# Decay on the attention output, a closer second layer, new planning figures, and load tiles kept at multiples of 256 bytes, in a fused attention and MLP kernel

## The chip, the cores and the metric

The kernel runs on one core of one Trainium2 chip. The metric is the device time of one execution in microseconds (us). An execution counts as slow when it took over 1.5% longer than the fastest of the same kernel. Ratios and profiles use runs in the fast state alone. Three executions were in the slow state (one of e2 at 218.12 us, one of e3 at 216.13, one of the kernel before at 751.23); they are in the medians and ranges that I quote, not in the ratios. The profile covers a slightly shorter stretch than the timed run (span 212.4 us against 214.5 us timed), so spans are compared with spans and times with times. In the profile's lines PE is TensorE (PEld its weight loads), DVE VectorE, ACT ScalarE, POOL GpSimd, and a q behind a name is that engine's sequencer. SBUF and PSUM are the memories that the kernel's tiles lie in; every matmul here writes its result to PSUM. An eviction is the copy of such a result from PSUM to SBUF.

## The reference, cut to what matters

```python
batch, n_heads, seq, head_dim = (4, 8, 768, 64); block = 64
rel = pos[:, None] - pos[None, :]
Dmask = np.where(rel >= 0, lam[:, None, None] ** rel[None, :, :], 0.0)
# for each block of the sequence:
intra = np.einsum('bhic,bhjc->bhij', qb, kb) * Dmask[None]
intra = np.einsum('bhij,bhjd->bhid', intra, vb)
inter = np.einsum('bhid,bhde->bhie', qb * lam_pow[None], kv_state)
out[:, :, sl] = intra + inter
kv_state = lam_block * kv_state + np.einsum('bhsd,bhse->bhde', kb * rev_pow[None], vb)
# then an MLP on x = attention output, 3072 x 512 -> 2048 -> 512
h = x @ w_in
g = np.where(h >= 1, h, np.where(h <= -1, 0.0, (h + 1) ** 2 / 4))
y = g @ w_out
```

The decay lam^(i-j) is a product of a factor of the query's position, lam^i, and one of the key's, lam^(-j). The kernel multiplies V (which carries the key's index) by the key's factor on GpSimd. The query's factor belongs to one row of the result, so it may be applied to the query or, just as well, to the finished output row. That freedom is what the change uses.

## The kernel before

There are 24 blocks of 128 tokens. The first six are transposed on TensorE, the 18 later ones by a DMA. Their outputs become xT, the input of layer 1: 96 groups of matmuls (16 of 128 columns each for the first three of six stages, then 8 of 256). Layer 2 has 96 groups of four matmuls of 512 columns (the last four groups in two pieces each). Between the layers ScalarE makes r = relu(h+1), and VectorE makes t = min(r/2, 1), w = r - t and gT = w*t, one set for every two layer-1 groups.

```python
def f_qn(c):        # query of a later block, scaled on VectorE: two SBUF inputs
    nc.vector.tensor_tensor(kq[c % NKQ][:, 2 * HP:, :]..., qkv_ld[c, 0],
                            _bc(tab_n[:, c % NCB, :], 2, D), op=AX.mult)
def f_qT(c):        # query of one of the first six blocks, scaled out of PSUM
    nc.vector.tensor_tensor(qT[c], ptt[c][1], tab_q[:, c % NCB], op=AX.mult)
def f_m(c, g):      # mask of the scores, PSUM times SBUF -> sc
    ...
def f_o(c):         # output matmuls, po <- sc,vi and the state's part
    ...
def f_x(c):         # eviction of the attention output, plain copy on ScalarE
    nc.scalar.copy(out=xT[sx][:, :, off:off + C], in_=pot[c])
```

No engine's program is written down in order. Every operation is added to a list with its planned duration, what it needs and when it is due; a list scheduler runs over these planned times and emits each engine's instructions in the order that comes out. A changed duration in the plan therefore moves real instructions.

```python
l_seq = [(1,) + x for x in l1_order[:FO]]        # FO = 16 layer-1 groups first
for i in range(len(l2_order)):                   # then one of each in turn
    l_seq.append((2,) + l2_order[i])
    if i + FO < len(l1_order):
        l_seq.append((1,) + l1_order[i + FO])
...
# in the scheduler: where TensorE is planned to wait, it gets matmuls on zeros
for _ in range(int((t - pe_end - 60) // (216 if t > 8000 else 430))):
    nc.tensor.matmul(spin, lhsT=idle[:, 0:128], rhs=idle, start=True, stop=True)
```

The last loop makes the "fillers": matmuls whose result nobody reads.

## Time and profile before

| | before |
|---|---|
| time, median of 3 runs | 213.78 us (213.44 to 214.03) |
| span of the profile | 212.4 us |
| busy: TensorE, VectorE, ScalarE, GpSimd | 205.3, 160.2, 150.4, 116.1 us |
| VectorE between 45 and 104 us | 55.92 of 59.00 us |
| gaps of TensorE after 18.3 us | 2.14 us |
| fillers after 18 us | 4 |

The page's summary of the chain that ended last is the first thing to read, as shares of the span by engine:

```profile
PE 66%; DVE 21%; DMA 6%; issue 3%; POOL 2%; ACT 1%; POOLq 0%; DVEq 0%
```

VectorE holds 21% of the chain. That says how long one could walk back through VectorE's instructions, not how much time is lost there: the chain may go along whichever of two full engines happens to end last. The lines that show how little TensorE really loses are in the prediction.

### The profile page before, as it was taken

The numbers are of one execution on the slowest core, as the hardware profiler recorded it, in microseconds if no ns is written. First come the engines' busy times: TensorE is split into PE (matmuls) and PEld (weight loads), VectorE is DVE, ScalarE is ACT, GpSimd is POOL, SyncE is SP. The second block draws the span as 40 slices with busy tenths as digits, with TensorE's granted clock in tenths as the row PEclk, the third lists the DMA queues.
The fourth block names the chain that finished last, engine by engine and source line by source line (L and its number), as shares of the span: only waits on it lengthen the run. The fifth ranks groups of instructions, "written<-read, shape, count | busy, mean of one in ns | idle before, by whom it ended". The sixth has DMA issues, their size and how long they took to land.

```text
span 212.4 us, 5710 instructions
## 1 busy us (share of the span) xinstructions
PE 205.3 (97%) x2324; PEld 146.7 (69%) x2324; DVE 160.2 (75%) x240; ACT 150.4 (71%) x306; POOL 116.1 (55%) x148
## 2 busy tenths in 40 slices
PE   7899999999999999999999999999999999999994
PEld 2476987676649788779677767667767776666442
DVE  6627887899997999999999999798769546364200
ACT  5899785498749898868789887795977664444120
POOL 8998636159998798687377586673835000000000
PEclk9999999999999999999999999999999999999999
DMA  5999999999999999894997969978861400110112
GB/s 143 258 224 244 213 262 265 220 219 189 269 274 261 253 216 155 205 257 104 204 229 172 205 142 235 221 167 198 205 154 43 124 25 27 49 49 34 68 49 99
DMA packets 95737, 36.80 MB, mean 173 GB/s; under 512 B 87392, under 2 KB 91744, under 8 KB 95712
## 3 DMA queue, kind: packets, MB, share of 16 engines
q1 hardware_dynamic: 90064, 28.06, 58.6%
q0 software_dynamic: 5504, 8.39, 18.3%
q8 instruction: 18, 0.29, 0.6%
q14 instruction: 7, 0.06, 0.1%
q10 hardware_dynamic: 144, 0.00, 0.0%
HBM read 27.27 MB, written 6.29 MB: 158 GB/s over the span
## 4 chain that ended last, share of the span: by engine, by line
PE 66%; DVE 21%; DMA 6%; issue 3%; POOL 2%; ACT 1%; POOLq 0%; DVEq 0%
PE ph L385 29%; PE py L430 29%; DVE w L403 5%; DVE gT L418 4%; DVE t L399 4%; DVE kq L276 4%; DMA w_in_sb<-in_moe_w_in_dram 4%; DVE kq L273 2%; DMA x1f<-in_k_dram 2%; DVE sc L348 2%; PE po L368 2%; PE pu L324 1%; PE po L366 1%; PE ps L341 1%; POOL vn L287 1%
## 5 line engine op out<-in xcount | busy, mean ns | idle before, releaser
L385 PE MATMUL ph<-xT,w_in_sb 128*128 128x128 bf16 (+1 forms) x1152 | 97.3, 237 | 0.3 <-DMA w_in_sb<-in_moe_w_in_dram 0.3
L430 PE MATMUL py<-w_out_sb,gT 128*128 128x512 bf16 (+2 forms) x400 | 95.0, 371 | 0.0
L385 PEld LDWEIGHTS <-w_in_sb 128*128 128x128 bf16 x1152 | 80.7, 98 | 14.2 <-DMA w_in_sb<-in_moe_w_in_dram 0.8
L393 ACT ACTIVATE r<-ph,one 128x512 bf16<-128x512 f32 x96 | 65.3, 687 | 32.3 <-PE ph L385 21.0
L290 POOL TENSOR_TENSOR vn<-x2f,tab_k 64x256 bf16<-64x256 f32 x72 | 57.2, 794 | 33.4 <-DMA x2f<-in_v_dram 17.6
L430 PEld LDWEIGHTS <-gT 128*128 128x128 bf16 x400 | 35.6, 98 | 27.9
L399 DVE TENSOR_SCALAR t<-r 128x1024 bf16<-128x1024 bf16 x48 | 28.8, 601 | 20.4 <-ACT r L393 20.1
L418 DVE TENSOR_TENSOR gT<-w,t 128x1024 bf16<-128x1024 bf16 x48 | 39.6, 824 | 1.3
L403 DVE TENSOR_TENSOR w<-r,t 128x1024 bf16<-128x1024 bf16 x48 | 39.0, 812 | 1.4
L327 ACT CAST ubd<-pu 64x256 bf16<-64x256 f32 x76 | 27.7, 364 | 5.4 <-PE pu L324 4.6
L293 POOL COPY vi<-vn 64x512 bf16<-64x512 bf16 x36 | 29.7, 824 | 2.0
L436 ACT COPY osb<-py 128x512 f32<-128x512 f32 (+1 forms) x24 | 13.9, 580 | 13.5 <-PE py L430 12.8
L271 ACT CAST kq<-x1f 64x256 bf16<-64x256 f32 x54 | 21.7, 401 | 0.6
L375 ACT CAST xT<-po 128x512 bf16<-128x512 f32 x24 | 14.0, 584 | 3.4 <-PE po L368 3.2
L276 DVE TENSOR_TENSOR kq<-x0f,tab_n 128x512 bf16<-128x512 f32 x18 | 15.9, 883 | 0.3
L348 DVE TENSOR_TENSOR sc<-ps,causal 128x512 bf16<-128x512 f32 x18 | 12.3, 682 | 2.0 <-PE ps L341 1.9
L241 PE MATMUL py<-idle 128*128 128x512 bf16 x36 | 11.9, 441 | 1.2 <-DVE one L119 1.2
L368 PE MATMUL po<-sc,vi 128*128 128x64 bf16 x144 | 10.5, 193 | 1.4 <-DVE sc L348 1.3
L273 DVE TENSOR_TENSOR kq<-x1f 64x256 bf16<-64x256 f32 x18 | 11.1, 618 | 0.5
L366 PE MATMUL po<-xq,ubd 128*128 128x64 bf16 x132 | 10.6, 193 | 0.0
L366 PEld LDWEIGHTS <-ubd 128*128 128x128 bf16 x132 | 8.9, 98 | 2.0 <-issue 1.3
L368 PEld LDWEIGHTS <-vi 128*128 128x128 bf16 x144 | 9.1, 98 | 1.6 <-issue 0.6
(63 smaller groups left out, 124.4 us busy)
## 6 DMA issues: line engine op xcount, KB each, us to landing
out_dram<-osb SPq DMA_DIRECT2D x23, 256.0 KB, 2.5
x1f<-in_k_dram SPq DMA_DIRECT2D x19, 256.0 KB, 3.4
x0f<-in_q_dram SPq DMA_DIRECT2D x19, 256.0 KB, 3.9
x2f<-in_v_dram SPq DMA_DIRECT2D x18, 256.0 KB, 3.9
w_in_sb<-in_moe_w_in_dram POOLq DMA_DIRECT2D x4, 512.0 KB, 8.9
w_out_sb<-in_moe_w_out_dram POOLq DMA_DIRECT2D x4, 512.0 KB, 11.8
x2f<-in_v_dram POOLq DMA_DIRECT2D x6, 256.0 KB, 7.4
x1f<-in_k_dram POOLq DMA_DIRECT2D x5, 256.0 KB, 7.8
```

Source lines behind the costliest of these rows:

```text
L271: nc.scalar.copy(out=o, in_=i)
L276: nc.vector.tensor_tensor(kq[c % NKQ][:, 2 * HP:, :].rearrange("p a (b d) -> p (a b) d", b=2), qkv_ld[c, 0], _bc(tab_n[:, c % NCB, :], 2, ...
L290: nc.gpsimd.tensor_tensor(vn[c % NV][HD[hi], HP * g:HP * g + HP, :], quarter(qkv_ld[c, 2], g, hi), _bc(tab, 2, D), op=AX.mult)
L293: nc.gpsimd.tensor_copy(vi[c % NV][HD[hi], :, HD[hi]], vn[c % NV][HD[hi]])
L327: nc.scalar.copy(out=ubd[(2 * c + j) % NUB][HD[hi], :, HD[hi]], in_=pu[0][HD[hi], :, HD[hi] if c < NCB else HD[0]])
L368: nc.tensor.matmul(po[:, hp, HD[j]], lhsT=vi[c % NV][:, HP * j + hp, :], rhs=sc_sb[c, 1][:, hp, HD[j]], start=(cb == 0 and j == 0), stop=True)
L385: nc.tensor.matmul(ph[:, j * m:(j + 1) * m], lhsT=w_in_sb[:, ko, (i + j) * 128:(i + j + 1) * 128], rhs=xT[s][:, ko, p * m:(p + 1) * m], st ...
L393: nc.scalar.activation(out=r_t[grp][:, i, :], in_=ph_t[s, ni, part], func=AF.Relu, bias=one[:, 0:1])
L399: nc.vector.tensor_scalar(t_t[grp], r_t[grp], 0.5, 1.0, op0=AX.mult, op1=AX.min)
L403: nc.vector.tensor_tensor(w_t[grp], r_t[grp], t_t[grp], op=AX.subtract)
L418: nc.vector.tensor_tensor(o, w, t, op=AX.mult)
L430: nc.tensor.matmul(t[:, j], lhsT=gT[s][:, ko, ms * 128:(ms + 1) * 128], rhs=w_out_sb[:, ko, j], start=(ko == 0), stop=(ko == FO - 1))
```

## The change

The change has three parts, which the experiments below name D, L and P; the alignment of the load tiles belongs to D.

- **D, decay**: VectorE no longer scales the query. ScalarE casts it (in the first six blocks VectorE copies it out of PSUM), and the eviction of the attention output, now on VectorE, multiplies by the decay table. The small table tab_n goes, and padding is trimmed so that the load tiles stay at multiples of 256 bytes.
- **L, closer layer 2**: layer 1 runs 16 groups ahead at first; the lead shrinks to 8 by the end.
- **P, planning**: hand shifts, planned durations, landing times of loads, slack and the plan's model of VectorE and GpSimd slowing each other.

```diff
 # D
-    nc.vector.tensor_tensor(kq[...], qkv_ld[c, 0], _bc(tab_n[:, c % NCB, :], 2, D), op=AX.mult)
+    nc.scalar.copy(out=kq[...], in_=qkv_ld[c, 0])
-    nc.vector.tensor_tensor(qT[c], ptt[c][1], tab_q[:, c % NCB], op=AX.mult)
+    nc.vector.tensor_copy(qT[c], ptt[c][1])
-    nc.scalar.copy(out=xT[sx][:, :, off:off + C], in_=pot[c])
+    nc.vector.tensor_tensor(xT[sx][:, :, off:off + C], pot[c], tab_q[:, c % NCB], op=AX.mult)
-    tab_n = const.tile([128, NCB, H], F32)
-    const.tile([128, 52], F32, name="pad1")
+    const.tile([128, 36], F32, name="pad1")
 # L (cut; it replaces the loop over l2_order shown above)
+    LAG = 8
+    for i, x in enumerate(l1_order):
+        l_seq.append((1,) + x)
+        n = i + 1 - FO + (FO - LAG) * max(0, i + 1 - FO - 0) / (len(l1_order) - FO - 0)
+        while n2 < n:
+            l_seq.append((2,) + l2_order[n2]); n2 += 1
 # P (cut)
-    SHIFT = {("tab", 4, 1): 69000, ("g1", 7): -58500, ("cast", 3, 2): 38400}
+    SHIFT = {("cv", 6, 0, 0): 74500, ("y", 0): -14800, ("r", 1): -136800, ("tab", 2, 3): -110900, ("zv", 1): -1000}
-    if e == "DVE" and t < pool_end: ...
+    if e == "DVE" and t < pool_end and x.key[0] in ("g1", "g2", "g", "ki"): ...
-    lat = 1500 if u.eng == "PE" and x.end > 66000 ...
+    lat = 1500 if u.eng == "PE" and x.end > 48000 ...
+    LX = {('w', 0): 800, ('ld', 2, 1): 1000, ...}     # planned landing times
 ...
```

More of the change, by code (lines that the diff above doesn't have):

```diff
@@ L53 @@
     CPS = MS // C
-    SHIFT = {("tab", 4, 1): 69000, ("g1", 7): -58500, ("cast", 3, 2): 38400}
+    SHIFT = {("cv", 6, 0, 0): 74500, ("y", 0): -14800, ("r", 1): -136800, ("tab", 2, 3): -110900, ("zv", 1): -1000}
     PLAIN, KA, WIDE = 6, 2, 6
     CUT = 384
-    LD, RING, VBN, VCN = 6, 6, 740, 730
+    LD, RING, VBN, VCN = 6, 6, 800, 760
     KE = ('ACT', 'ACT', 'ACT', 'DVE')
@@ L206, in run_plan @@
                 x.due = x.own
+        for x in ops:
             x.due += SHIFT.get(x.key, 0)
@@ L218, in run_plan @@
             ns = x.ns
-            if e == "DVE" and t < pool_end:
-                if x.key[0] == "g1":
-                    ns += pool_end - t
-                elif x.key[0] in ("g2", "g"):
-                    ns += min(ns, (pool_end - t) / 2)
-            if e == "POOL":
+            if e == "DVE" and t < pool_end and x.key[0] in ("g1", "g2", "g", "ki"):
+                ns += min(pool_end - t, 400) if x.key[0] == "g1" else min(300, (pool_end - t) * 0.4)
+            if e == "POOL" and x.key[0] in ("cv", "vb", "cast", "zv"):
                 pool_end = t + ns
@@ L231, in run_plan @@
                 if left[u.key] == 0:
-                    lat = 1500 if u.eng == "PE" and x.end > 66000 and u.key[0] in "sou" else SLACK if u.eng == "PE" and x.end > 30000 else DSLACK if u.eng == "SP" else LAT
+                    lat = 1500 if u.eng == "PE" and x.end > 48000 and u.key[0] in "sou" else SLACK if u.eng == "PE" and x.end > 30000 else DSLACK if u.eng == "SP" else LAT
                     rel = o_due(u.key[1]) - 14000 if u.key[0] == "t" and u.key[1] >= CPS else o_due(u.key[1]) - 20000 if u.key[0] == "xt" and u.key[1] >= CPS else o_due(u.key[1]) - 26000 if u.key[0] == "li" and u.key[1] > SW else 0
@@ L275, in f_qn @@
     def f_qn(c):
-        nc.vector.tensor_tensor(kq[c % NKQ][:, 2 * HP:, :].rearrange("p a (b d) -> p (a b) d", b=2), qkv_ld[c, 0],
-                                _bc(tab_n[:, c % NCB, :], 2, D), op=AX.mult)
+        nc.scalar.copy(out=kq[c % NKQ][:, 2 * HP:, :].rearrange("p a (b d) -> p (a b) d", b=2), in_=qkv_ld[c, 0])
     def f_xt(c):
@@ L461 @@
         l2_order += [(s, ms, kg) for ms, kg in o]
-    l_seq = [(1,) + x for x in l1_order[:FO]]
-    for i in range(len(l2_order)):
-        l_seq.append((2,) + l2_order[i])
-        if i + FO < len(l1_order):
-            l_seq.append((1,) + l1_order[i + FO])
+    LAG = 8
+    l_seq, n2 = [], 0
+    for i, x in enumerate(l1_order):
+        l_seq.append((1,) + x)
+        n = i + 1 - FO + (FO - LAG) * max(0, i + 1 - FO - 0) / (len(l1_order) - FO - 0)
+        while n2 < n:
+            l_seq.append((2,) + l2_order[n2])
+            n2 += 1
+    l_seq += [(2,) + x for x in l2_order[n2:]]
     l_due = {x: T0 + i * STEP for i, x in enumerate(l_seq)}
@@ L482, in f_load @@
             tc.add_manual_dep(d.ins, w_dma[GATE[c]].ins.name, SYNC)
+    LX = {('w', 0): 800, ('ld', 2, 1): 1000, ('ld', 2, 0): 1000, ('ld', 2, 2): 2300, ('w', 1): 1900, ('ld', 3, 1): 1900, ('ld', 3, 0): 1900, ('ld', 3, 2): 3100, ('w', 2): 2800, ('w', 3): 2500, ('w', 4): 1200, ('ld', 4, 1): 1200, ('ld', 4, 0): 1300, ('ld', 4, 2): 2100, ('w', 5): 1800, ('w', 6): 500, ('ld', 5, 1): 700, ('ld', 5, 0): 700, ('ld', 5, 2): 1500, ('w', 7): 2500}
     SW = 6
@@ L509 @@
             add(key, "SP" if sp else "POOL", 600 if sp and i == 0 else 640 if sp else 900 if kind == "c" else 800, fn, need, due=0, extra=1250 if sp else 930)
-            add(land, "DMA", ns, lambda: None, [key] + landed[-1:], extra=950 if sp and i == 0 else 1000 if kind == "c" and i < 2 else 2400 if kind == "c" and i < SW else 2200 if kind == "w" else 2000, due=0)
+            add(land, "DMA", ns, lambda: None, [key] + landed[-1:], extra=LX[land] if land in LX else 950 if sp and i == 0 else 1000 if kind == "c" and i < 2 else 2400 if kind == "c" and i < SW else 2200 if kind == "w" else 2000, due=0)
             landed.append(land)
@@ L517 @@
     add(("tabk",), "ACT", 250, lambda: nc.scalar.activation(out=tab_k, in_=arg, func=AF.Exp, scale=-1.0))
-    add(("off",), "ACT", 2 * 230, f_off, [("tab", 0, 3)])
-    add(("tabn",), "ACT", 250, lambda: nc.scalar.activation(out=tab_n, in_=arg, func=AF.Exp), [("x", PLAIN - 3)])
+    add(("off",), "ACT", 2 * 145, f_off, [("tab", 0, 3)])
     for c in range(NCH):
@@ L529 @@
                 [("ld", c, x), ("t", c - 3), ("u", c - 3, 1), ("cast", c - 1, x)])
-        for hp in range(HP) if P and c % 2 == 0 else ():
-            add(("tab", c, hp), "ACT", 410, lambda c=c, hp=hp: tabq(c, hp), [("tab", c, hp - 1), ("off",) if c else None, (None, ("kb", 0), ("x", 1))[c // 2]])
+        for hp in range(HP) if c < NCB and c % 2 == 0 else ():
+            add(("tab", c, hp), "ACT", 510 if c else 410, lambda c=c, hp=hp: tabq(c, hp), [("tab", c, hp - 1), ("off",) if c else None, (None, ("kb", 0), ("x", 1))[c // 2]])
         free = [("xt", c - NKQ), ("u", c - NKQ, 0), ("u", c - NKQ, 1), ("zk", c % NKQ)]
@@ L535 @@
                 for hi in range(2):
-                    add(("ki", c, g, hi), KE[2 * g + hi], 401 if KE[2 * g + hi] == "ACT" else 540, lambda c=c, g=g, hi=hi: f_ki(c, g, hi), [("ld", c, 1)] + free, due=od - 16000)
-            add(("qn", c), "DVE", 750, lambda c=c: f_qn(c), [("ld", c, 0), ("tabn",)] + free, due=od - 16000)
+                    add(("ki", c, g, hi), KE[2 * g + hi], 401 if KE[2 * g + hi] == "ACT" else 430, lambda c=c, g=g, hi=hi: f_ki(c, g, hi), [("ld", c, 1)] + free, due=od - 16000)
+            add(("qn", c), "ACT", 615, lambda c=c: f_qn(c), [("ld", c, 0)] + free, due=od - 16000)
         fv = [("ld", c, 2), ("tabk",), ("o", c - NV), ("u", c - NV, 0), ("u", c - NV, 1), ("vb", c - NV, 0), ("vb", c - NV, 1)]
@@ L548 @@
             add(("kb", c), "ACT" if c < KA else "DVE", 590 if c < KA else 430, lambda c=c: f_kb(c), [("t", c), ("s", c - 2, 0), ("s", c - 2, 1)])
-            add(("qT", c), "DVE", 690, lambda c=c: f_qT(c), [("t", c), ("o", c - 3), ("qT", c - 1)] + [("tab", c // 2 * 2, hp) for hp in range(HP) if c < NCB])
+            add(("qT", c), "DVE", 430, lambda c=c: f_qT(c), [("t", c), ("o", c - 3), ("qT", c - 1)])
         else:
@@ L562 @@
             if c >= WIDE or h == 0:
-                add(("s", c, h), "PE", mm(*[128] * 4) if P else mm(*[64] * 8), lambda c=c, h=h: f_s(c, h),
+                add(("s", c, h), "PE", 190 + mm(*[128] * 4) if P else mm(*[64] * 8), lambda c=c, h=h: f_s(c, h),
                     [("kb", c), ("qT", c), ("xd", c), ("m", c, 0) if h and P else ("m", c - 1, 1), ("m", c - 1, 0)],
@@ L567 @@
         ub = [("ub", c - 1, 1, hi) for hi in range(2) if cb] + [("ub", c, 0, hi) for hi in range(0 if P else 2)]
-        add(("o", c), "PE", mm(*[128] * (4 if cb else 0), *[128] * 4) if P else mm(*[64] * (16 if cb else 12)), lambda c=c: f_o(c),
+        add(("o", c), "PE", 190 + mm(*[128] * (4 if cb else 0), *[128] * 4) if P else mm(*[64] * (16 if cb else 12)), lambda c=c: f_o(c),
             [("m", c, 1), ("vb", c, 0), ("vb", c, 1), *ub, ("x", c - 1), ("o", c - 1)], due=od, extra=FILL)
-        add(("x", c), "ACT", 600, lambda c=c: f_x(c), [("o", c), ("x", c - 1), ("l1", (c // CPS - 2) * FO + FO - 1)])
+        add(("x", c), "DVE", 690, lambda c=c: f_x(c), [("o", c), ("x", c - 1), ("l1", (c // CPS - 2) * FO + FO - 1)] + [("tab", c // 2 * 2, hp) for hp in range(HP) if c < NCB])
     n_of = {x: n for n, x in enumerate(l1_order)}
@@ L581 @@
         if j == RW - 1:
-            add(("g1", grp), "DVE", 360, lambda grp=grp: f_g1(grp), [("r", n1), ("g", grp - 3)])
-            add(("g2", grp), "DVE", 640, lambda grp=grp: f_g2(grp), [("g1", grp), ("g", grp - 3)])
-            add(("g", grp), "DVE", 640, lambda a=l1_order[n1 - 1], b=(s, i, p): f_g3(a, b),
+            add(("g1", grp), "DVE", 420, lambda grp=grp: f_g1(grp), [("r", n1), ("g", grp - 3)])
+            add(("g2", grp), "DVE", 690, lambda grp=grp: f_g2(grp), [("g1", grp), ("g", grp - 3)])
+            add(("g", grp), "DVE", 690, lambda a=l1_order[n1 - 1], b=(s, i, p): f_g3(a, b),
                 [("g2", grp), ("g", grp - 1), ("l2", (s - 1) * FO - 1)])
```

## The prediction

> **What bounds the kernel now.** I read the busy table by stage first (columns: stretch, its length, then busy us and instruction count of PE, PEld, DVE, ACT, POOL, then TensorE clock, DMA share, GB/s).
>
> ```profile
> 0.00:18.30 18.30, 15.71 (x145) 8.53 (x146) 10.62 (x27) 14.87 (x34) 17.02 (x25) 1.00 0.92 215
> 18.30:45.00 26.70, 26.70 (x388) 21.63 (x388) 21.79 (x38) 18.60 (x35) 12.78 (x17) 1.00 1.12 232
> 45.00:104.00 59.00, 57.64 (x818) 43.73 (x816) 55.92 (x71) 47.93 (x103) 48.33 (x60) 1.00 1.05 222
> 104.00:160.00 56.00, 56.00 (x598) 41.10 (x596) 49.28 (x70) 45.70 (x96) 35.82 (x46) 1.00 0.86 192
> 160.00:212.40 52.40, 49.26 (x391) 31.69 (x387) 22.62 (x38) 23.32 (x41) 2.10 (x2) 1.00 0.16 53
> ```
>
> TensorE is busy from 18.3 us on, and in one stage, 45 to 104, VectorE is nearly as full (55.92 of 59.00). Then the chain that ended last, in order of time, at the places where it changes hands:
>
> ```profile
> 2.48 4.58 DMA x1f<-in_k_dram
> ...
> 10.62 7.62 DMA w_in_sb<-in_moe_w_in_dram
> ...
> 18.28 1.96 PE ph L385 x32
> ...
> 44.71 1.28 DVE sc L346 x2
> ...
> 103.86 1.79 PE ph L385 x32
> ...
> 195.41 13.87 PE py L430 x80
> ```
>
> Loads lead to 18.28 us (the second quarter of w_in), TensorE to 44.7, VectorE (with a little "issue") to about 103.9, TensorE to the end. A chain through VectorE says who ended last, not how much TensorE lost. For that I took, from the start times in the trace, each distance between consecutive matmul starts less columns/2.4 ns. After 18.28 us only five excesses are over 0.1 us: 0.53 at 61.4, 0.26 at 65.9, 0.64 at 86.9, 0.12 at 95.0, 0.59 at 103.3: together 2.14 us. All are before the output matmul po<-sc,vi, which needs the masked scores from VectorE. The waits of TensorE in that stage show three of them (less what its queue hides), and the one row there is:
>
> ```profile
> PE po L368 <- DVE sc L348: 1.3, 3, 0.5
> ```
>
> Some sixteen more gaps of about 0.095 us stand where matmuls change their tile of the array; the change leaves those. Four filler matmuls (0.213 us each, 0.85 in all) still run after 18.28. So TensorE loses about 3.0 us that a better schedule could return. This ceiling is the main fact of the prediction: 3.0/213.78 = 1.4%, unless the first 18.3 us or the tail get shorter.
>
> **What the Trainium skill says.** "Perfetto Trace Analysis", section Identifying the Most-Contended Engine, warns that matmul busy time is a poor measure of headroom, because matmuls are pipelined. The trace agrees: busy reads 57.64 of 59.00 in the stage where 2.14 us are lost; hence the start distances.
>
> "SBUF — State Buffer", section Who interferes with whom: a VectorE instruction with two SBUF inputs contends with a GpSimd instruction that reads SBUF; one with at most one SBUF input, outside the two-port modes, does not. The trace agrees. VectorE's groups between 45 and 104 us:
>
> ```profile
> L403 DVE TENSOR_TENSOR w<-r,t 128x1024 bf16<-128x1024 bf16 x14 | 12.7, 906 | 0.3
> L276 DVE TENSOR_TENSOR kq<-x0f,tab_n 128x512 bf16<-128x512 f32 x10 | 10.0, 1004 | 0.2
> ...
> L348 DVE TENSOR_TENSOR sc<-ps,causal 128x512 bf16<-128x512 f32 x8 | 5.4, 679 | 0.8 <-PE ps L341 0.8
> ```
>
> The query scaling (two SBUF inputs) takes 1004 ns; over the whole run it lies between 678 and 1102. The mask (PSUM times SBUF, same shape and types) takes 679. After 170 us, with GpSimd idle, w takes 692 instead of 906.
>
> "VectorE: DVE Perf Modes", section Why PSUM operands drop a tier: an fp32 PSUM operand holds the operation to 1x. So the new scaling xT<-po,tab_q should cost what the mask costs, 0.68 us; I use that measured value.
>
> "DMA: Bandwidth & Descriptors", section How a descriptor splits into AXI transactions: a transfer that does not start at a multiple of 256 bytes pays an extra transaction. I looked up where the load tiles lie in both built programs: the first k tile starts at byte 92416 before and 92160 after, 361 and 360 times 256. Both are aligned. Dropping tab_n (192 bytes) and 64 bytes of padding moves everything by exactly 256. No run here shows an unaligned tile; this part only keeps what was there, and I give it zero.
>
> **The change part by part.**
>
> 1. Query scaling, later blocks (18 blocks). VectorE loses qn (mean 883 ns over all 18, 1004 in the tight stage) and gains the scaled eviction (about 0.685). In the tight stage: ten qn leave, 10.0 us; nine evictions arrive (nine of the old ScalarE ones lie there), 9 x 0.685 = 6.2 us. Net -3.8 us of VectorE work. ScalarE loses the plain eviction (584 ns) and gains a cast of 0.615: +0.03 x 18 = +0.6 us, beside other work.
>
> 2. First six blocks. qT becomes a copy (like kT<-pt, 425 ns) instead of 681: -0.26 x 6 = -1.5 us. The eviction comes to VectorE: +0.685 x 6 = +4.1. Net +2.6 us, mostly before 45 us, where VectorE has 26.70 - 21.79 = 4.9 us free and the loads or TensorE set the end. ScalarE loses 6 x 0.584 = 3.5 us there, two of them in its fullest stretch.
>
> 3. Layer 2 closer. Before, layer-1 groups stay 16 ahead of layer 2. Now 80 remaining layer-1 groups are spread over 88 layer-2 groups, so the lead shrinks to 8. TensorE's sum is the same. The tight stage held 450/16 = 28 layer-1 groups beside 28 of layer 2; at 80:88 it holds some 2.5 fewer, or 1.3 fewer sets of t, w, gT at 0.71 + 0.91 + 0.96 = 2.57 us: -3.3 us of VectorE work, moved to after 160 us, where it has 30 us free. At the end, 52 matmuls instead of 80 follow the last layer-1 group, by the order of the built programs. The first that needs its result has four layer-2 groups before it, 4 x 0.86 = 3.4 us. The chain r, t, w, gT took 195.44 to 198.04 = 2.6 us. It fits, with 0.8 us to spare.
>
> 4. Order. Fillers fall from 36 to 27; after the second w_in quarter from four to two, -0.43 us. On GpSimd two casts move up one place past a load issue; the second w_in quarter keeps its place behind the same work, so I expect 18.3 us again.
>
> Sum: VectorE in the tight stage goes from 55.9 to about 55.9 - 3.8 - 3.3 = 48.8 us of 58, about 84% instead of 95%. It should stop setting the end there. I let 80% of the 2.14 us go, -1.7, and -0.4 for fillers. The eviction on VectorE puts an operation that waits for TensorE into an in-order queue: in several places of the new order only one short operation stands between mask and eviction, so VectorE will sometimes idle; I charge +0.2 us of new stalls. Net -1.9: 213.78 - 1.9 = 211.9.
>
> **Rivals.**
> - VectorE becomes the bound through its queue: mask, output matmul, eviction alternate between TensorE and VectorE, and the single po buffer waits for the eviction. For: ScalarE's old eviction waited 3.2 us in four cases for po, and VectorE would now stand idle. Against: the freed 7 us. It would leave TensorE's stalls or double them: 213.5 to 216.
> - The load chain moves. A shift in POOL's order or in the 18.3 us start carries through one for one: DMA is full there (share 0.92 to 1.12). For: two casts change places. Against: same transfers, same issue place. Either way within 1 us: 211 to 213.
> - All stalls and fillers go and ScalarE's relief starts layer 1 earlier: 213.78 - 3.0 = 210.8; beyond 2% (below 209.5) needs at least 1.3 us from the start, which the w_in landing blocks.
> - Tail exposed: if the last gT takes over 3.4 us, each extra 0.1 us is paid in full; the end sits 3.1 us after the last matmul either way.
>
> **Range and chances.** 211.9, with 210.2 to 213.6 as 8 in 10: the low end is every stall gone plus some start, the high end is the stalls replaced by others. The ceiling of 3.0 us keeps over 2% faster unlikely: 0.07. Slower by over 2% needs 4 us of new stalls: 0.02. Within 2%: 0.91.
>
> **What would show it.** Right: the chain no longer runs through VectorE between 45 and 104 us; xT<-po,tab_q takes 0.67 to 0.70 us whatever GpSimd does; gaps before po<-sc,vi sum to under 0.6 us; the first group on the second w_in quarter starts at 18.3 +/- 0.5; layer 2 alone lasts about 13.87 - 28 x 0.213 = 7.9 us at the end without a gap. Wrong: a start of layer 1 moved by over a microsecond, new matmul gaps behind xT or gT, or gT at the tail arriving late.

## The result, and the profile after

| | before | after |
|---|---|---|
| time, median (range, runs) | 213.91 us (213.44 to 214.78, 4) | 211.70 us (211.15 to 212.52, 4) |
| span of the profile | 212.4 us | 209.9 us |
| end of the last matmul | 209.26 us | 206.79 us |

The ratio is 0.9895, with a 95% interval of 0.9849 to 0.9942: 1% faster, and within 2%. Here and below a ratio is the mean time of one kernel's fast runs over that of the other's of the same rounds, so it is not quite the ratio of the medians that stand beside it. The new kernel itself was timed in these four runs only; an experiment is compared with it through the two ratios to the kernel before.

The chain that ended last, by engine, in the profile after:

```profile
PE 92%; DMA 4%; POOL 2%; issue 1%; DVE 0%; POOLq 0%; DVEq 0%
```

VectorE has left the chain. In order of time it reads, at its first hand-over and at its end (start, length, what):

```profile
5.10 7.38 DMA w_in_sb<-in_moe_w_in_dram
12.53 1.07 PE ph L381 x16
...
198.98 7.83 PE py L426 x52
```

A load leads to 12.5 us, where layer 1 starts; from there the chain stays on TensorE, but for "issue" (time in which the engine waited for nothing that the profile shows, 1% of the span in many small pieces), to the last 52 matmuls of layer 2. The busy table by stage, with the same columns as in the prediction:

```profile
0.00:18.30 18.30, 13.77 (x138) 8.12 (x141) 10.74 (x28) 13.93 (x31) 17.45 (x26) 1.00 0.94 226
18.30:45.00 26.70, 26.43 (x403) 22.36 (x403) 25.45 (x43) 18.34 (x34) 13.73 (x17) 1.00 1.12 228
45.00:104.00 59.00, 58.37 (x822) 44.44 (x830) 53.87 (x72) 49.46 (x106) 48.05 (x62) 1.00 1.14 231
104.00:160.00 56.00, 55.48 (x550) 39.63 (x558) 43.68 (x65) 42.67 (x88) 29.72 (x36) 1.00 0.70 168
160.00:209.90 49.90, 46.47 (x381) 31.14 (x386) 26.07 (x41) 24.09 (x44) 7.19 (x11) 0.99 0.24 71
```

In this table TensorE looks less busy than it was: this profile lacks 33 of the program's 2315 matmul records (the weight loads, second figure, are complete). A missing record of 512 columns leaves a hole of about 0.218 us, which I don't count as a gap. With those set aside, the start distances show after 18.3 us two excesses of 0.10 us (at 42.6 and 47.6), hardly more than the gaps of some 0.095 us at a change of tile, where the kernel before lost 2.14 us. The waits of TensorE in that stage, which before held the one row for po, have no row at all.

Where the 2.5 us of span went, then: 2.14 us of gaps, less the 0.2 that came back, 0.43 us of two fillers fewer, 0.14 us of an earlier second quarter of w_in (its first matmul at 18.14 instead of 18.28 us). That is the 2.5 us. After the last matmul both kernels need 3.1 us.

VectorE's groups between 45 and 104 us (count, busy us, mean ns, idle before and who ended it):

```profile
L399 DVE TENSOR_TENSOR w<-r,t 128x1024 bf16<-128x1024 bf16 x15 | 14.2, 945 | 0.4
L414 DVE TENSOR_TENSOR gT<-w,t 128x1024 bf16<-128x1024 bf16 x15 | 13.1, 876 | 0.3
...
L371 DVE TENSOR_TENSOR xT<-po,tab_q 128x512 bf16<-128x512 f32 x9 | 6.2, 684 | 3.5 <-PE po L364 3.4
```

The scaled eviction takes 684 ns beside a busy GpSimd, where the query scaling took 1004. VectorE stands idle 3.4 us for po, as the first rival of the prediction feared, yet TensorE does not wait: those idle times fit into what VectorE now has to spare.

### The profile page after: what moved, and what is told of

Same layout as the page of the kernel before. It is cut to its first block, busy times and chain, and to the rows that moved or that the text cites. A ratio compares the mean times of both kernels' runs of the same rounds, so it can differ in the third digit from the quotient of the medians.

```text
span 209.9 us, 5652 instructions
## 1 busy us (share of the span) xinstructions
PE 200.5 (96%) x2282; PEld 145.7 (69%) x2315; DVE 159.8 (76%) x246; ACT 148.5 (71%) x299; POOL 116.1 (55%) x148
## 3 DMA queue, kind: packets, MB, share of 16 engines
q0 software_dynamic: 5504, 8.39, 18.3%
## 4 chain that ended last, share of the span: by engine, by line
PE 92%; DMA 4%; POOL 2%; issue 1%; DVE 0%; POOLq 0%; DVEq 0%
PE ph L381 41%; PE py L426 39%; DMA w_in_sb<-in_moe_w_in_dram 4%; PE pu L320 2%; PE po L364 2%; PE ps L337 2%; PE po L362 2%; PE py L238 1%; POOL x2f L480 1%; PE pt L298 1%; PE po L356 1%; PE ps L332 1%; PE po L352 1%; POOL x1f L480 0%; POOL x0f L480 0%
## 5 line engine op out<-in xcount | busy, mean ns | idle before, releaser
L426 PE MATMUL py<-w_out_sb,gT 128*128 128x512 bf16 (+2 forms) x369 | 90.1, 370 | 1.7 <-issue 0.2
L381 PEld LDWEIGHTS <-w_in_sb 128*128 128x128 bf16 x1152 | 80.8, 98 | 15.8 <-DMA w_in_sb<-in_moe_w_in_dram 1.2
L286 POOL TENSOR_TENSOR vn<-x2f,tab_k 64x256 bf16<-64x256 f32 x72 | 55.4, 770 | 39.8 <-DMA x2f<-in_v_dram 35.8
L395 DVE TENSOR_SCALAR t<-r 128x1024 bf16<-128x1024 bf16 x48 | 29.6, 617 | 22.3 <-ACT r L389 21.9
L399 DVE TENSOR_TENSOR w<-r,t 128x1024 bf16<-128x1024 bf16 x48 | 39.6, 825 | 1.4
L289 POOL COPY vi<-vn 64x512 bf16<-64x512 bf16 x36 | 30.4, 843 | 2.0
L371 DVE TENSOR_TENSOR xT<-po,tab_q 128x512 bf16<-128x512 f32 x24 | 16.5, 686 | 10.0 <-PE po L364 7.3
L283 POOL TENSOR_TENSOR vn<-x2f,tab_k 128x512 bf16<-128x512 f32 x6 | 7.6, 1264 | 6.9 <-DMA x2f<-in_v_dram 6.8
L273 ACT CAST kq<-x0f 128x512 bf16<-128x512 f32 x18 | 11.1, 616 | 0.3
L320 PEld LDWEIGHTS <-kq 128*128 128x128 bf16 x132 | 7.8, 98 | 3.9
```

Of the source, the lines that this page charges most:

```text
L286: nc.gpsimd.tensor_tensor(vn[c % NV][HD[hi], HP * g:HP * g + HP, :], quarter(qkv_ld[c, 2], g, hi), _bc(tab, 2, D), op=AX.mult)
L289: nc.gpsimd.tensor_copy(vi[c % NV][HD[hi], :, HD[hi]], vn[c % NV][HD[hi]])
L371: nc.vector.tensor_tensor(xT[sx][:, :, off:off + C], pot[c], tab_q[:, c % NCB], op=AX.mult)
L381: nc.tensor.matmul(ph[:, j * m:(j + 1) * m], lhsT=w_in_sb[:, ko, (i + j) * 128:(i + j + 1) * 128], rhs=xT[s][:, ko, p * m:(p + 1) * m], st ...
L395: nc.vector.tensor_scalar(t_t[grp], r_t[grp], 0.5, 1.0, op0=AX.mult, op1=AX.min)
L399: nc.vector.tensor_tensor(w_t[grp], r_t[grp], t_t[grp], op=AX.subtract)
```

## The experiments

All ran in three groups, each on one chip with runs of the kernel before on the same chip (its medians 214.01, 214.33 and 214.29 us). A profile is one execution, and the spans of the kernel before alone lie between 211.2 and 213.5 us, so a single profile's start is not a kernel's typical one. "Gaps" are the excesses of TensorE's start distances that the prediction defines, between 45 and 110 us. "Start" is the first matmul on the second quarter of w_in. The rival theories were: VectorE's load makes the gaps (T1), the order of the operations or the in-order queue makes them (T2), the start or the loads make the difference (T3).

### e1: the kernel before with the query scaling off VectorE

```diff
# before
-    nc.vector.tensor_tensor(kq[...], qkv_ld[c, 0], _bc(tab_n[...], 2, D), op=AX.mult)
+    nc.scalar.copy(out=kq[...], in_=qkv_ld[c, 0])
```

The plan is untouched, so TensorE's order is the same as before, instruction for instruction. The result is wrong on purpose (the decay is missing).

> The kernel before with TensorE's order unchanged, instruction for instruction; only the query scaling of the 18 later blocks leaves VectorE and becomes a plain cast on ScalarE (the decay of those blocks is lost, so the result is wrong on purpose). Theory A, VectorE's load makes TensorE wait before po: the five gaps before po (2.14 us together) fall to under 0.6 us and the time falls by 1.3 to 2.2 us, to about 212. Theory B, the gain of the change comes from its new order and closer layer 2, not from VectorE's load: the gaps stay at 1.5 us or more and the time falls by less than 0.6 us.

Measured: 212.21 us (212.19 to 212.23, 6 runs), ratio 0.9919 [0.9895, 0.9943], span 210.1. One gap of 0.26 us is left; before, it was five with 2.14. VectorE between 45 and 104 us falls from 55.92 to 50.90:

```profile
45.00:104.00 59.00, 58.91 (x844) 44.88 (x842) 50.90 (x64) 53.88 (x115) 47.87 (x61) 1.00 1.16 229
```

With the order of TensorE unchanged, this shows that VectorE's load made the gaps (1.88 of 2.14 us). Part of the gain, 0.5 us, came from a start at 17.77 instead of 18.28.

### e2: the new kernel with an instruction of the removed scaling's size put back on VectorE

```diff
# after, in f_qn of each later block
     nc.scalar.copy(out=kq[...], in_=qkv_ld[c, 0])
+    nc.vector.tensor_tensor(extra, qkv_ld[c, 0], qkv_ld[c, 0], op=AX.max)
```

> The changed kernel with TensorE's order unchanged, plus one useless VectorE instruction in each of the 18 later blocks, of the removed query scaling's size and with two SBUF inputs (a 128x512 float32 maximum into a scratch tile), so about 0.7 to 1.0 us each, some ten of them between 45 and 104 us. Theory A: VectorE is full again in that stage, gaps of 1.5 to 3 us come back before po or the layer-2 matmuls, and the time rises by 1.5 to 3 us to about 213.5. Theory B: VectorE has the room, the time rises by less than 0.6 us.

Measured: 216.03 us (214.59 to 218.12, 10), ratio 1.0084 [1.0053, 1.0115]; 1.9% over the new kernel by the ratios (1.0084/0.9895). TensorE's order is again the same. The extra instruction took 889 ns in the tight stage. The gaps are back and, with 4.14 us, larger than the 1.5 to 3 us that theory A expected. The evictions stay on VectorE too, so this run asks more of it than the kernel before did (173.0 us busy in all against 160.2): it shows the direction, not the size. The longer of the two waits of TensorE that stand between 45 and 110 us names the mask again (the other, 0.8 us, is layer 1 waiting for ScalarE's r):

```profile
PE po L367 <- DVE sc L347: 2.4, 2, 1.5
```

So the load works in both directions: e1 takes it out of the old order and the gaps go, e2 puts it into the new order and they come. T2 alone can't explain either. The windows from 45 to 64 us show what "full" means here, first the new kernel, then e2, which has the same order (the third pair is VectorE, the second the weight loads):

```profile
45.00:64.00 19.00, 18.84 (x216) 12.47 (x216) 16.30 (x21) 14.31 (x32) 16.80 (x22) 1.00 1.13 249
```

```profile
45.00:64.00 19.00, 17.39 (x180) 10.63 (x178) 18.73 (x23) 13.10 (x28) 16.67 (x20) 1.00 1.14 240
```

With 16.30 of 19 us VectorE leaves TensorE alone; with 18.73, TensorE does 178 weight loads instead of 216 in the same time, with 1.94 us of the gaps in this stretch.

### e3: the new kernel with the old distance of layer 2

```diff
-    LAG = 8
+    LAG = 16
```

This leaves D and P together (the sequence is that of before to within one place).

> The changed kernel with layer 2 again 16 layer-1 groups behind (the scheduler then places everything anew). My prediction gave the closer layer 2 some 3.3 us of VectorE work moved out of the tight stage, but the decay alone should be nearly enough: time 0 to 0.8 us longer than the changed kernel, VectorE in 45 to 104 us busier by 2 to 3 us. Rival, the closer layer 2 is what made the gain: 1.5 to 2.2 us longer, with gaps before po back at 2 us.

Measured: 212.62 us (211.07 to 216.13, 7), ratio 0.9918 [0.9884, 0.9952], no gap. Its fast runs lie between 211.07 and 213.04; the profiled one was the fastest and started at 16.99 us, over a microsecond earlier than the new kernel, with no change to the loads. The run's expectation also had VectorE busier by 2 to 3 us between 45 and 104 us without the closer layer 2; it was less busy, 52.56 us against 53.87. The closer second layer is therefore not needed to close the gaps once D and P are there; on top of them it is worth 0.2% (0.9918 to 0.9895), which these intervals don't separate from nothing.

### e4: the new kernel with its load tiles 64 bytes off

```diff
-    const.tile([128, 36], F32, name="pad1")
+    const.tile([128, 52], F32, name="pad1")
```

> The changed kernel with 64 bytes more padding, so that the load tiles start 64 bytes past a multiple of 256; order unchanged. If the alignment matters as the Trainium skill's page on DMA says for transfers that do not start at a multiple of 256 bytes, the landings of the loads of 256-byte rows take longer (hundreds of ns to a microsecond more from issue to landing), the first layer-1 group starts later than 12.5 us and the time rises by 0.5 to 3 us. If it doesn't matter: within 0.3 us of the changed kernel and the same landing times.

Removing tab_n without mending the padding would have given this layout. All orders are identical to the new kernel's. Measured: 213.94 us (213.90 to 214.09, 14), ratio 0.9991 [0.9971, 1.0010]: the whole gain is gone. No gap stands between 45 and 110 us. The start moved to 20.15 us, 2.0 later, and the span grew by 2.1 (212.0). The loads on the page, issue to landing in the last figure, first of the new kernel and then of e4:

```profile
x1f<-in_k_dram SPq DMA_DIRECT2D x19, 256.0 KB, 3.7
...
w_in_sb<-in_moe_w_in_dram POOLq DMA_DIRECT2D x4, 512.0 KB, 8.1
```

```profile
x1f<-in_k_dram SPq DMA_DIRECT2D x19, 256.0 KB, 4.5
...
w_in_sb<-in_moe_w_in_dram POOLq DMA_DIRECT2D x4, 512.0 KB, 9.2
```

In the first 12.5 us the DMA engines moved 180 GB/s instead of 225 at the same busy share of 0.87. The page that the prediction cites tells of this extra transaction for what a descriptor reads. In this run the place in SBUF that a load writes moved, and with it all that lies behind the padding, the tiles of the weights included. So the run shows that the offset costs 2.1 us, and not that this transaction is the cause. Keeping the tiles at multiples of 256 bytes is a condition of the change's success and not a gain.

### e5, e6, e7: each part alone on the kernel before

The edits are the diff's lines of D alone, L alone and P alone.

> The kernel before with the moved decay alone: old distance of layer 2, old planning figures and shifts of the scheduler. If the moved decay is the cause: the gaps before po (2.14 us before) fall under 0.8 us, VectorE in 45 to 104 us falls by 2 to 4 us, and the time is 1.3 to 2.2 us below the kernel before. Rival, the retuned scheduler is what made it: the gaps stay or grow, because the evictions now queue on VectorE where the old plan did not expect it, and the time stays within 0.6 us of the kernel before or rises.

> The kernel before with the closer layer 2 alone. My prediction charged it with 3.3 us less VectorE work in the tight stage: then the gaps fall by about half, to 1 us, and the time by 0.5 to 1.2 us. Rival, after the run with 16 groups of lead: it does nothing, the gaps stay at 2 us and the time within 0.5 us of the kernel before.

> The kernel before with the scheduler's new planning figures and shifts alone (decay on the query as before, layer 2 at its old distance). If order and planning made the gain: gaps before po under 0.8 us and the time 1.3 to 2.2 us below the kernel before. If VectorE's load made it: gaps of 1.2 us or more stay, and the time is within 0.8 us of the kernel before.

Measured:

- e5 (D): 214.00 us (213.45 to 215.05, 22), ratio 0.9995 [0.9982, 1.0009]. Nothing gained: the rival expectation was the right one.
- e6 (L): 212.68 us (212.41 to 213.22, 6), ratio 0.9914 [0.9892, 0.9937]. One gap of 0.88 us left, and a start at 17.85. That is more than the 0.5 to 1.2 us expected, and nearly the ratio of the whole change: by these intervals ([0.9849, 0.9942] for the whole) L alone can't be told from it.
- e7 (P): 216.01 us (214.41 to 216.87, 17), ratio 1.0055 [1.0035, 1.0074]. A loss that neither expectation had (0.55% is 1.2 us, against "within 0.8 us"), with a single gap of 2.12 us at 62.3 in that stretch, and one more of 0.73 us at 124.5, both before po.

The gaps of e5 still sum to 1.83 us, but they have moved. The waits of its TensorE between 45 and 110 us:

```profile
PE ph L383 <- DVE xT L373: 1.0, 2, 0.6
```

Layer 1 now waits for the new eviction. The work saved on the query did not reach the stretch that was full: from 45 to 64 us VectorE is busy 18.48 of 19 us in e5, against 18.64 before (first the kernel before, then e5):

```profile
45.00:64.00 19.00, 18.64 (x208) 12.14 (x206) 18.64 (x22) 14.00 (x31) 17.61 (x23) 1.00 1.18 247
```

```profile
45.00:64.00 19.00, 17.58 (x205) 11.97 (x206) 18.48 (x23) 15.12 (x34) 17.68 (x23) 1.00 1.15 257
```

The first rival of the prediction (mask, output, eviction in one queue) comes true here. In e1 the scaling taken off VectorE gained 0.8% under the same planning figures, so what takes the gain away in e5 is the eviction that came to VectorE, or the order that the scheduler made with it; no run separates the two.

### e8 and e10: pairs of parts

e8 is D and L under the old planning, e10 is L and P without D.

> The kernel before with the moved decay and the closer layer 2, under the old planning figures and shifts. If the closer layer 2 is what relieves VectorE whatever else is done: like the run with the closer layer 2 alone, a ratio to the kernel before of 0.988 to 0.993. If the moved decay needs the new planning (the evictions queue on VectorE between 45 and 64 us, where it was 97% busy with the decay moved alone): layer-1 matmuls wait for xT, gaps of 1.5 us or more, ratio 0.994 to 1.0.

> The changed kernel without the moved decay: query scaling on VectorE as before, closer layer 2, new planning. If the moved decay has a share in the gain once the planning knows of it: 0.996 to 1.004 of the kernel before, VectorE over 96% busy between 45 and 64 us, gaps of 1.5 us or more. If the closer layer 2 alone makes the gain: 0.988 to 0.993.

Measured: e8 213.86 us (213.39 to 216.10, 22), ratio 0.9983 [0.9967, 1.0000]; e10 213.20 us (212.70 to 214.51, 19), ratio 0.9955 [0.9939, 0.9971]. In e8 layer 1 waits for xT as in e5, with gaps of 1.88 us: adding D to L under the old plan loses what L had gained, as its second expectation had it. e10 met neither of its expectations: its ratio lies just below the first's range, and its one gap is 0.78 us and not 1.5 or more. All eight combinations are now there, the whole with none being the kernel before:

| parts | run | ratio to before | gaps 45 to 110, us | VectorE busy 45 to 64, of 19 us |
|---|---|---|---|---|
| none | before | 1 | 2.14 | 18.64 |
| D | e5 | 0.9995 | 1.83 | 18.48 |
| L | e6 | 0.9914 | 0.88 | 18.61 |
| P | e7 | 1.0055 | 2.12 | 18.65 |
| D and L | e8 | 0.9983 | 1.88 | 18.09 |
| L and P | e10 | 0.9955 | 0.78 | 18.45 |
| D and P | e3 | 0.9918 | 0 | 14.57 |
| all | after | 0.9895 | 0.10 | 16.30 |

Only where D and P meet does VectorE fall clearly below 18 of 19 us in this stretch, and only there do the gaps vanish (but for 0.10 us). P alone costs 0.55%, D alone gives nothing, both together give 0.82%. The gains are not a sum: D and L together, under the old plan, are worth less than L alone. Gaps don't explain every difference in time. The start differs too between these profiles (16.99 us in e3 to 18.48 in e5), and so together they do: the span less the start and less all gaps after it is 191.6 to 192.1 us in each of the eight. Of L's gain as much as 0.4 us may be a start that another execution would not have.

### e9: the kernel before with its tiles at a multiple of 512 bytes

```diff
# before
-    const.tile([128, 52], F32, name="pad1")
+    const.tile([128, 116], F32, name="pad1")
```

> The kernel before with everything behind the padding moved by 256 bytes: its load tiles, at an odd multiple of 256 before, then lie at a multiple of 512, as those of the changed kernel do. If only the multiple of 256 counts: within 0.4 us of the kernel before. If a part of the gain is this: 0.5 to 1.5 us faster, with the first layer-1 group starting earlier.

Measured: 214.80 us (213.35 to 215.69, 22), ratio 1.0009 [0.9992, 1.0026]. The start came 0.5 us earlier (17.77), but the gaps between 45 and 110 us grew to 3.36 us, and the span is 213.1. All instruction orders are those of the kernel before, and its waits for the mask rose from 1.3 to 2.1 us: in this execution the earlier start was more than given back. In e1, with VectorE relieved, a start just as early was kept. A coarser alignment than 256 bytes gained nothing in the kernel before.

### i3 and i2: what is left of the start

i3 drops the fillers planned after 12.5 us. i2 does so too, and loads the second quarter of w_in directly behind the first.

```diff
# after, i3 and i2
-    for _ in range(int((t - pe_end - 60) // (216 if t > 8000 else 430))):
+    for _ in range(int((t - pe_end - 60) // (216 if t > 8000 else 430)) if t < 12500 else 0):
# i2 only
-    order = [("c", 0), ("c", 1), ("w", 0), ("c", 2), ("w", 1), ("c", 3), ("w", 2), ...]
+    order = [("c", 0), ("c", 1), ("w", 0), ("w", 1), ("c", 2), ("w", 2), ("c", 3), ...]
```

> An attempt to beat both: the changed kernel without the nine filler matmuls planned after the first layer-1 group. In its profile the chain ran through fillers at 13.65, 14.8 and 17.7 us, so work whose data was there stood behind them. If so, layer 1 on the second w_in quarter starts 0.3 to 1.0 us earlier than 18.14 us and the time falls by as much, to 210.7 to 211.4. If the loads set that start, nothing changes; if the granted clock falls without them, the time rises.

> A second attempt: as the run without late fillers, and the second w_in quarter is loaded before block 2 of q, k and v instead of behind it. Four layer-1 groups then need only blocks 0 and 1, so TensorE should have real work earlier: the 33rd layer-1 matmul at 16.0 to 17.0 us, time 0.5 to 1.5 us below the changed kernel. Against: block 2 lands about 4 us later, and TensorE waits for it at 18 to 20 us: then no gain, or a loss of up to 1.5 us.

Measured, i3: 210.84 us (210.32 to 212.50, 6), ratio 0.9841 [0.9807, 0.9874], correct, span 208.6: the fastest kernel of the study. Its interval overlaps that of the new kernel, and they ran in different rounds, so that it beats the new kernel is likely and not settled. Its start was 16.88 us, but that of e3, with fillers, was 16.99; part of it may be the luck of the landings.

Measured, i2: 217.32 us (216.53 to 218.40, 6), ratio 1.0135 [1.0101, 1.0168]. The second quarter of w_in was in use at 15.69 us, 2.5 us earlier than in the new kernel, and the loads that had to give way made TensorE wait for the attention of later blocks: the "against" of its expectation, but with a loss larger than the 1.5 us named there. Then came something else. The windows of i2 (PE is the first pair, TensorE's clock the third figure from the end):

```profile
18.00:20.00 2.00, 1.14 (x21) 0.96 (x18) 1.93 (x4) 2.00 (x5) 2.00 (x4) 1.00 1.07 336
20.00:22.00 2.00, 0.73 (x12) 0.65 (x13) 1.97 (x6) 1.79 (x5) 1.70 (x2) 1.00 1.19 218
22.00:24.00 2.00, 1.21 (x13) 0.90 (x13) 1.92 (x4) 0.00 (x0) 2.00 (x3) 0.52 1.24 205
24.00:26.00 2.00, 2.00 (x22) 2.00 (x20) 1.12 (x3) 0.00 (x0) 2.00 (x3) 0.50 1.19 282
26.00:28.00 2.00, 2.00 (x23) 1.61 (x22) 1.12 (x2) 1.18 (x3) 1.16 (x2) 0.50 1.08 293
```

TensorE was busy less than half of 18 to 22 us (1.14 + 0.73 = 1.87 of 4), and from 22.1 to 28.9 us the granted clock was one half: TensorE is busy all of 24 to 28 us there with 45 matmuls. Half a clock over 6.8 us costs up to 3.4 us, by an estimate from these figures. The Trainium skill's page "TensorE: Matmul & The Clock Gate", section What's actually happening, says that the gate follows how busy TensorE has recently been and has two rates, full and half. The 0.50 agrees. i2 changes two things, so it doesn't tell whether fillers alone would have kept the clock; i3 without fillers kept 1.00 throughout, and its waits after 12.5 us were 0.7 us at the longest.

## Why the prediction was right, point by point

The time (211.70 measured, 211.9 predicted) and the class were right.

- **The ceiling.** The argument that no more than 3.0 us were to be had, because TensorE lost only 2.14 us in gaps and 0.85 in fillers, held: 2.5 us of span came. e1 reached the same floor in another way (span 210.1), and no combination of parts went below it except by an earlier start: e3's span of 208.7 us is 1.2 shorter than the new kernel's, and it started 1.15 us earlier.
- **VectorE off the path.** Right, and shown: no gap before po over 0.1 us, VectorE at 0% of the chain. That it was VectorE's load is shown by e1 and e2, in both directions and at the same order.
- **The eviction's cost.** Predicted from the mask, 0.67 to 0.70 us whatever GpSimd does; measured 0.676 to 0.692 us over all 24.
- **The start and the tail.** Start at 18.3 +/- 0.5: 18.14. Layer 2 at the end 7.9 us without a gap: 7.83 on the chain; the last r to gT took 2.6 us again and fitted.
- **Fillers.** Two fewer after 18 us, -0.43, as counted from the built program.
- **Alignment.** Given zero because both kernels are aligned, which is right as a difference. e4 shows that it guards 2.1 us. The prediction took the page's rule for one of any transfer; the page words it for reads, and gives one row that is off and needs no extra transaction. What e4 measured is a load's place in SBUF.

What was mis-sized, and one assumption that failed:

- **"VectorE in the tight stage ... 48.8 us of 58, about 84%."** Measured 53.87 of 59, 91%. The decay's term was right: ten query scalings (10.0 us) left, nine evictions (6.2) came. The term that failed is step 3's -3.3 us. That step took 2.5 layer-1 groups out of the stage and left layer 2 at 28 groups, as if TensorE would stand idle for them. Layer 1 did not thin out there: the stage holds 15 sets of t, w and gT (38.7 us) instead of 14 (36.0). By complete counts of weight loads, layer 1 has 449 between 45 and 104 us (447 before) and layer 2 has 120 (112): TensorE filled the stage with two more groups of layer 2 and no fewer of layer 1. e3 agrees: with the old distance VectorE has 52.56 us there, less than the new kernel's 53.87. (Under the old plan, e6, the closer layer 2 took off 1.75 us.) The relief of layer 1 came between 104 and 160 us: 223 weight loads instead of 257, and VectorE, which D relieves there too, at 43.68 instead of 49.28 us. The same counts show the lead itself: at 104 us layer 1 was 11.4 groups ahead before and 12.1 after, at 160 us 15.8 and 10.5. The difference that the step placed in the tight stage was not there yet.
- **"I let 80% of the 2.14 us go."** All went. **"+0.2 us of new stalls"** was 0.2.
- **Between 18.3 and 45 us** VectorE gained 3.7 us (25.45 against 21.79), predicted +2.6; harmless, as argued.
- **The sum D plus L.** I added the reliefs of VectorE as if each acted wherever I put it. The combinations refute that: D and L under the old plan give 0.17%, less than L alone (0.86%). The prediction gave the planning edits no share of their own beyond the order of fillers; in fact D is worth nothing without P, and P without D is a loss. P alone packs 3.2 us more VectorE work into 18.3 to 45 us (24.97 against 21.79; e10 does as well, without the loss). Its gaps after the start sum to 3.0 us instead of 2.14 (2.12, 0.73 and 0.19), which is nearly the 0.95 us that its span is longer. Which edit of P makes them is open; no run isolates it.

So the total came out right because it rested on the ceiling of TensorE, which doesn't depend on how VectorE's relief comes about; the account of the relief was right on D's cost and wrong on where L acts. A ceiling says what can't be exceeded, not that it is reached. By the prediction's sums D alone, with 3.8 us off VectorE in the tight stage, would have brought part of the gain, and it brought none (e5). That the whole change reached the ceiling was in this sense luck: the prediction gave no share to the planning without which D does not pay.

## What to carry to other kernels

Where two engines are nearly full, add up the gaps of the one that sets the end: that sum, and not the other engine's share of the chain, is the most that relief of the other can bring there. When an edit takes one operation off a full engine and puts another on it, the plan that orders that engine may decide whether it pays; test the edit and the plan as a pair, and each part alone, for one part (here L) may give nearly all. When a tile is removed, check where all later tiles now begin: 64 bytes cost this kernel as much as the whole change brought.

## What the Trainium skill lacked or had wrong

- "DMA: Bandwidth & Descriptors" states the extra transaction of an unaligned read but gives no time for it, nor for a load whose place in SBUF is off. Here, all tiles behind the padding 64 bytes off a multiple of 256 made a 256 KB load land after 4.5 us instead of 3.7 (medians of the k loads), moved 180 instead of 225 GB/s in the first 12.5 us, and cost 2.1 us of span (e4).
- "SBUF — State Buffer" has the rule of who contends with GpSimd, and it held, but for such a pair it has no size. In the kernel before, w (bf16, 128x1024, two SBUF inputs) took 692 ns on average in the 21 cases beside which no GpSimd instruction ran and 905 in the 27 others; t took 427 and 747; the mask, with one SBUF input, 687 and 681.
- "TensorE: Matmul & The Clock Gate" ties the return to half rate to an idle window of about 3.4 us; its section on a second failure mode says that frequent short idles can bring it too, without saying how much idling. In i2 the clock was halved at 22.1 us after four microseconds in which TensorE was busy 1.87 us, with no single wait between matmuls over 1.8 us.
- "Perfetto Trace Analysis" doesn't say that matmul records can be missing: the profile after has 2282 of 2315, and a missing one of 512 columns looks like a stall of 0.22 us.
